# A decode block on one Trainium2 core: part of the scores and wider value products on VectorE, a maximum of its own for each key group, heads normalised together

## The chip, the core and the metric

The kernel runs on one core of a Trainium2 chip. Its engines are TensorE (PE; its weight loads are PEld), VectorE (DVE), ScalarE (ACT), GpSimd (POOL) and SyncE (SP), which issues nearly all transfers here; 16 DMA engines move the data from HBM. The metric is the device time of one execution in microseconds. Where a time is given for the kernel before, it is the median of three runs; the profile is of one execution.

## The reference

One decoding step of a transformer block for a batch of B = 2, with one token each, all in fp32:

```python
x = A_x                                          # (2, 1, 448)
q = (layernorm(x) @ wq) -> 16 heads of 256
scores = einsum("bhqd,bhkd->bhqk", q, k_cache) * 256 ** -0.5     # 8192 keys
p = softmax(scores)
h = x + einsum("bhqk,bhkd->bhqd", p, v_cache) @ wo
n = layernorm(h)
out = h + ((n @ w_gate) * (n @ w_up)) @ w_down   # 448 -> 1792 -> 448
```

The caches are what is large: 2 x 16 x 8192 x 256 numbers each for K and V, 537 MB together. Every one of these numbers is used once.

## The kernel before, in words

The work is cut into 32 items, one per head and batch row, in the order item i = 2 h + b. For each, one 8 MB tile of K (`kt`, 64 KB per partition) and one of V (`vt`, the same) come in. K lies with the 256 feature dimensions as two chunks of 128 partitions and the 8192 keys as G = 4 groups of GK = 2048. V lies with partition = key group and value row r (R = 32), and NO = 8 columns of 2048 keys each.

There is one K buffer (pool `kbuf`), and there are two V buffers (pool `vbuf`). All loads are issued by SyncE in program order: wq, K0, V0, K1, V1, and so on (L84, L91). SyncE waits at each until its buffer is free, and everything behind stands behind it: K of item i + 1 waits until every reader of K of item i is done, V of item i + 1 until the products of item i - 1 are done. The order on every engine is the program's own; there is no scheduler.

For an item:

- `scores` (L201 to L209): 32 matmuls, 4 key tiles of 512 x 2 chunks x 4 groups. The four groups write to four blocks of 32 partitions of `s`, which holds the scores of all 8192 keys as 128 x 2048 in four PSUM banks. The 32 rows of a group are equal, as the query is repeated.
- VectorE takes the maximum along the keys (L242), PE transposes the 128 maxima (L244), VectorE takes their maximum (L246), PE spreads it to all partitions (L248), ScalarE copies it (L250).
- ScalarE computes p = exp(s - maximum), with the sum along the way (L252).
- VectorE multiplies each of the 8 columns of V by p and sums, in one instruction each with an accumulator (L259). These go back into the V buffer and are not read again; the sums are in `oacc`.

After both batch rows of a head `head_out` (L211 to L223) sums over partitions, divides by the sum of the exponentials and places the head in `oT`. It is issued after the scores of the next item.

After the last item, the K buffer takes wo in five loads, one V buffer the gate and up weights (`gu_t`, two and three loads), the other w_down (`wd_t`, five loads) (L265 to L278). Then: the output projection with wo (L292), the residual and the layer norm (L303 to L335), gate (L347), its scaling on ScalarE by the inverse variance (L348), up (L349), the product (L353), four transposes (L357), the product with w_down (L364), two copies and the output. g_ps and u_ps are two banks of one tile, `ff`.

Of the kernel before, what the change touches and what calls it, by code (L numbers as in the profile page):

```python
# [8 lines left out]
F32 = mybir.dt.float32  # L9
# [39 lines left out]
def tile_decode_block(  # L49
# [122 lines left out]

    qT = const.tile([P, 2, G, 2, 2, B], F32, name="qT")
    q_ps = ps_s.tile([P, 4, MM], F32, tag="s", name="q_ps")
    q_sb = one.tile([P, 2, MM], F32, tag="p", name="q_sb")
    for k in range(2):
        project(
            q_ps[:, k], wq_t, HD, (MM,) * 4, [k * BATCH + g * MM for g in range(4)],
# [9 lines left out]
            q_ps[:, 2 + k].rearrange("p (n g b r) -> p n g b r", n=4, g=G, b=B)[..., 0],  # L188
        )

    def queries(h):
        q = one.tile([P, 2, B, R], F32, tag="q", name=f"q_{h}")
        nc.scalar.activation(
            q.rearrange("p c b r -> p (c b) r"),
            qT.rearrange("p k g j c b -> p (k g j) (c b)")[:, h, :, None]
            .to_broadcast([P, 2 * B, R]),
            AF.Copy,
        )
        return q

    def scores(s, q, b, kt):  # L201
        for j in range(GK // MM):
            at = slice(j * MM, (j + 1) * MM)
            for c in range(2):
                for g in range(G):
                    nc.tensor.matmul(  # L206
                        s[g * R : (g + 1) * R, at], q[:, c, b, :], kt[:, c, g, at],
                        start=(c == 0), stop=(c == 1),
                    )  # L209

    def head_out(h, oacc, lsum):  # L211
        l_ps = ps_m.tile([P, B], F32, tag="sm", name=f"l_ps_{h}")
        nc.tensor.matmul(l_ps, ones, lsum, start=True, stop=True)  # L213
        rl = work.tile([P, B], F32, tag="rl", name=f"rl_{h}")
        nc.vector.reciprocal(rl, l_ps)  # L215
        oT_ps = ps_m.tile([P, B, 2], F32, tag="sm", name=f"oT_ps_{h}")
        for r in range(G):
            nc.tensor.matmul(
                oT_ps[r * R : (r + 1) * R], gsum, oacc[:, :, r::G], start=True, stop=True
            )  # L220
        nc.vector.tensor_mul(
            oT[:, h].rearrange("p c b -> p b c"), oT_ps, rl[:, :, None].to_broadcast([P, B, 2])
        )  # L223

    q_now = queries(0)
    last = None

    for i in range(NQ):
        h, b = divmod(i, B)
        kt = load_k(b, h)  # L230
        vt = load_v(b, h, 2 if i == NQ - 1 else 1)
        if b == 0:
            oacc = work.tile([P, B, NO], F32, tag="oacc", name=f"oacc_{h}")
            lsum = work.tile([P, B], F32, tag="lsum", name=f"lsum_{h}")

        s = ps_s.tile([P, GK], F32, tag="s", name=f"s_{i}")
        scores(s, q_now, b, kt)
        if last is not None:
            head_out(*last)
            last = None  # L240
        m = work.tile([P, 1], F32, tag="m", name=f"m_{i}")
        nc.vector.tensor_reduce(m, s, axis=AX.X, op=ALU.max)  # L242
        mT = ps_m.tile([1, P], F32, tag="sm", name=f"mT_{i}")
        nc.tensor.transpose(mT, m, ident)  # L244
        nm = work.tile([1, 1], F32, tag="nm", name=f"nm_{i}")
        nc.vector.tensor_reduce(nm, mT, axis=AX.X, op=ALU.max, negate=True)  # L246
        nb_ps = ps_m.tile([P, 1], F32, tag="sm", name=f"nb_ps_{i}")
        nc.tensor.matmul(nb_ps, ones[0:1, :], nm, start=True, stop=True)  # L248
        nb = work.tile([P, 1], F32, tag="nb", name=f"nb_{i}")
        nc.scalar.activation(nb, nb_ps, AF.Copy, scale=float(R))  # L250
        p = one.tile([P, GK], F32, tag="p", name=f"p_{i}")
        nc.scalar.activation(p, s, AF.Exp, bias=nb, scale=1.0, accum_out=lsum[:, b : b + 1])  # L252

        if b == B - 1 and h + 1 < H:
            q_now = queries(h + 1)

        for o in range(NO):
            v = vt[:, o, :]
            nc.vector.scalar_tensor_tensor(  # L259
                v, v, 1.0, p, op0=ALU.mult, op1=ALU.mult, accum_out=oacc[:, b, o : o + 1]  # L260
            )
        if b == B - 1:
            last = (h, oacc, lsum)
# [8 lines left out]
    def load_ff(t, w, cuts):  # L272
        for a, z in zip((0,) + cuts, cuts + (NF * D,)):
            nc.sync.dma_start(t[:, a:z], w[:, a:z])
# [7 lines left out]
    hm_ps = [ff[:, at, : 2 * P].rearrange("p (n k) -> p n k", k=P) for at in (2, 0)]  # L282
    ya_ps, yb_ps = ff[:B, 3, :YC], acc_ps[32 : 32 + B, :YC]
    for t in (g_ps, u_ps):
        nc.vector.memset(t[2 * 32 :, FG[2] :], 0.0)
# [9 lines left out]
                )  # L295

    project_out(range(WO_CUTS[1]))
    head_out(*last)
# [14 lines left out]
    hT = const.tile([P, DC, B], F32, name="hT")  # L313
    nc.vector.tensor_add(hT, xT, hT_ps)
    xc = center(hT, "h")
    for rows, c, to in LAYOUT:
        k = rows.stop - rows.start
        nc.vector.tensor_copy(  # L318
            xr[rows, to],
            xc[rows, c][:, :, :, None].to_broadcast([k, c.stop - c.start, B, 16]),  # L320
        )
# [14 lines left out]
    for ps, a, z in ((ya_ps, 0, YC), (yb_ps, YC, D)):  # L336
        at = a
        while at < z:
            c, k = divmod(at, P)
            n = min(P - k, z - at)  # L340
            nc.tensor.matmul(  # L341
                ps[:, at - a : at - a + n], hT[:, c, :], ident[:, k : k + n],
                start=(at == a), stop=False, skip_group_check=True,
            )
            at += n

    project_ff(g_ps, wg_t)  # L347
    nc.scalar.activation(g_sb, g_ps, AF.Copy, scale=rv)  # L348
    project_ff(u_ps, wu_t)  # L349
    hmT = const.tile([P, 4, 4, B], F32, name="hmT")  # L350
# [25 lines left out]
def pack(np, inputs):  # L376


    x = np.asarray(inputs["A_x"]).reshape(B, D).T
    last = x[3 * P :]  # L380
    got = {
        "x": np.concatenate(
            [x[: 3 * P].reshape(3, P, B).transpose(1, 0, 2).reshape(P, 3 * B),
             np.concatenate([last, last], axis=0)], axis=1
        )
    }
    k = np.asarray(inputs["A_k_cache"]).reshape(B, H, SK, 2, P)
    got["kc"] = np.ascontiguousarray(k.transpose(0, 1, 4, 3, 2)).reshape(B, H, P, 2 * SK)
# [45 lines left out]
```

## Time and profile before

| | us |
|---|---|
| median of three runs (1306.52 to 1307.53) | 1307.19 |
| the profiled execution's own time | 1306.09 |
| its span, first to last instruction | 1304.3 |
| VectorE busy | 663.4 |
| TensorE matmuls busy | 365.3 |
| ScalarE busy | 79.6 |
| mean granted TensorE clock, as a share | 0.631 |
| bytes moved by DMA (MB) | 561.59 |

The page is read with the program's names: `k<-in_kc_dram` is a K load, `s<-k,q` a score matmul, `v<-v,p` a value product. In a row of a group stand line, engine, operation, output and inputs, shapes and the count; then busy time and mean ns of one; then the engine's idle time just before these instructions and what ended it. In a row of a timeline stand start, duration, engine, line and operation, and in brackets the idle time before and its releaser. One matmul of fp32 shows as two records. In a row of a table of windows stand the window, its length, the busy time of PE, PEld, VectorE, ScalarE and GpSimd, then the granted TensorE clock, the share of the DMA engines and GB/s.

### The profile page before, as it was taken

The numbers are of one execution on the slowest core, as the hardware profiler recorded it, in microseconds if no ns is written. First come the engines' busy times: TensorE is split into PE (matmuls) and PEld (weight loads), VectorE is DVE, ScalarE is ACT, GpSimd is POOL, SyncE is SP. The second block draws the span as 40 slices with busy tenths as digits, with TensorE's granted clock in tenths as the row PEclk, the third lists the DMA queues.
The fourth block names the chain that finished last, engine by engine and source line by source line (L and its number), as shares of the span: only waits on it lengthen the run. The fifth ranks groups of instructions, "written<-read, shape, count | busy, mean of one in ns | idle before, by whom it ended". The sixth has DMA issues, their size and how long they took to land.

```text
span 1304.3 us, 6274 instructions
## 1 busy us (share of the span) xinstructions
PE 365.3 (28%) x2592; PEld 116.9 (9%) x2592; DVE 663.4 (51%) x648; ACT 79.6 (6%) x119; POOL 0.8 (0%) x7
## 2 busy tenths in 40 slices
PE   3333212332212233211232211323321233321247
PEld 1000000010000001000010000101000010100012
DVE  0246564445565445655444656444556544556552
ACT  0100000000000000000000000000000000000000
POOL 0000000000000000000000000000000000000000
PEclk9666566666556666656666655666655666655669
DMA  9999999999999999999999999999999999999998
GB/s 418 421 446 421 446 423 444 425 442 427 440 428 437 433 434 435 432 435 434 432 437 430 439 428 441 426 443 424 445 422 446 423 445 422 445 424 444 424 425 340
DMA packets 11841, 561.59 MB, mean 431 GB/s; under 512 B 1443, under 2 KB 1573, under 8 KB 2597
## 3 DMA queue, kind: packets, MB, share of 16 engines
q1 hardware_dynamic: 11668, 561.19, 99.5%
q8 instruction: 20, 0.33, 0.1%
q14 instruction: 9, 0.07, 0.0%
q10 hardware_dynamic: 144, 0.00, 0.0%
HBM read 561.19 MB, written 0.00 MB: 430 GB/s over the span
## 4 chain that ended last, share of the span: by engine, by line
DMA 75%; PE 24%; issue 0%; DVE 0%; SPq 0%; ACT 0%; ACTq 0%; DVEq 0%
DMA k<-in_kc_dram 73%; PE s L206 23%; DMA wo_t<-in_wo_dram 2%; PE ff_ps L167 1%; PE ff_ps L364 0%; SPq L267 0%; PE hT_ps L309 0%; PE acc_ps L292 0%; PE ff_ps L357 0%; PE l_ps L213 0%; DVE tail L353 0%; ACT tail L348 0%; DVE tail L303 0%; DVE xr L318 0%; PE acc_ps L341 0%
## 5 line engine op out<-in xcount | busy, mean ns | idle before, releaser
L259 DVE SCALAR_TENSOR_TENSOR v<-v,p 128x2048 f32<-128x2048 f32 x256 | 569.0, 2288 | 215.6 <-DMA v<-in_vc_dram 212.6
L206 PE MATMUL s<-k,q 128*32 128x512 f32 x2048 | 294.4, 739 | 804.2 <-DMA k<-in_kc_dram 804.2
L242 DVE TENSOR_REDUCE m<-s 128x1 f32<-128x2048 f32 x32 | 73.2, 2287 | 190.2 <-PE s L206 190.2
L206 PEld LDWEIGHTS s<-k,q 128*32 128x32 f32 x2048 | 80.9, 133 | 991.5 <-issue 991.5
L215 DVE RECIPROCAL rl<-l_ps 128x2 f32<-128x2 f32 x16 | 2.7, 171 | 166.7 <-PE l_ps L213 166.7
L250 ACT ACTIVATE nb<-nb_ps 128x1 f32<-128x1 f32 x32 | 5.5, 172 | 1148.3 <-PE nb_ps L248 1148.3
L252 ACT ACTIVATE p<-s,nb 128x2048 f32<-128x2048 f32 x32 | 63.0, 1968 | 1.0
L244 PE MATMUL mT<-ident,m 128*1 128x128 f32 x32 | 9.8, 306 | 79.4 <-DVE m L242 79.4
L259 DVE DVE_READ_ACCUMULATOR v<-v,p 128x1 f32 x256 | 21.3, 83 | 0.0
L248 PE MATMUL nb_ps<-nm,ones 1*128 1x1 f32 x64 | 15.2, 303 | 11.8 <-DVE nm L246 11.8
L246 DVE TENSOR_REDUCE nm<-mT 1x1 f32<-1x128 f32 x32 | 8.9, 278 | 12.7 <-PE mT L244 12.7
L248 PEld LDWEIGHTS nb_ps<-nm,ones 1*128 1x128 f32 x64 | 12.4, 241 | 19.1 <-DVE nm L246 19.1
L292 PE MATMUL acc_ps<-wo_t,oT 128*2 128x448 f32 x64 | 9.2, 632 | 14.6 <-DMA wo_t<-in_wo_dram 14.6
L244 PEld LDWEIGHTS mT<-ident,m 128*1 128x1 f32 x32 | 2.5, 79 | 96.1 <-DVE m L242 96.1
L167 PE MATMUL q_ps<-wq_t,xr 128*32 128x512 f32 x64 | 9.2, 727 | 2.3 <-DMA wq_t<-in_wq_dram 1.9
L167 PE MATMUL ff_ps<-gu_t,xr 128*32 128x384 f32 (+1 forms) x64 | 8.7, 633 | 0.9 <-ACT tail L348 0.9
L118 DVE TENSOR_REDUCE sum_h_x<-xT 128x2 f32<-128x6 f32 x1 | 0.2, 159 | 14.4 <-DMA xT<-in_x_dram 14.4
L186 DVE COPY qT<-q_ps 128x32 f32<-128x32 f32 x2 | 0.4, 191 | 12.0 <-PE q_ps L183 12.0
L252 ACT ACTIVATION_READ_ACCUMULATOR p<-s,nb 128x1 f32 x32 | 6.2, 193 | 0.0
L213 PE MATMUL l_ps<-lsum,ones 128*128 128x2 f32 x32 | 6.1, 262 | 0.0
L213 PEld LDWEIGHTS l_ps<-lsum,ones 128*128 128x128 f32 x32 | 4.8, 188 | 13.3 <-issue 13.3
L353 DVE TENSOR_TENSOR tail<-ff_ps,tail 128x256 f32<-128x256 f32 x2 | 0.8, 420 | 9.8 <-PE ff_ps L167 9.8
(69 smaller groups left out, 60.8 us busy)
## 6 DMA issues: line engine op xcount, KB each, us to landing
v<-in_vc_dram SPq DMA_DIRECT2D x2, 4096.0 KB, 37.8
wq_t<-in_wq_dram SPq DMA_DIRECT2D x1, 7168.0 KB, 19.4
wo_t<-in_wo_dram SPq DMA_DIRECT2D x1, 2688.0 KB, 16.2
wo_t<-in_wo_dram SPq DMA_DIRECT2D x1, 2240.0 KB, 21.2
gu_t<-in_B_w_gate_dram SPq DMA_DIRECT2D x1, 1792.0 KB, 28.9
gu_t<-in_B_w_up_dram SPq DMA_DIRECT2D x1, 1792.0 KB
wd_t<-in_wd_dram SPq DMA_DIRECT2D x2, 896.0 KB, 19.8
wo_t<-in_wo_dram SPq DMA_DIRECT2D x1, 1344.0 KB, 23.9
```

Of the source, the lines that this page charges most:

```text
L167: nc.tensor.matmul(ps[32 * g : 32 * g + 32, : wide[g]], xs.rearrange("p b r -> p (b r)"), w[:, at : at + wide[g]], start=(c == 0), stop=(c ...
L206: nc.tensor.matmul(s[g * R : (g + 1) * R, at], q[:, c, b, :], kt[:, c, g, at], start=(c == 0), stop=(c == 1),)
L213: nc.tensor.matmul(l_ps, ones, lsum, start=True, stop=True)
L215: nc.vector.reciprocal(rl, l_ps)
L242: nc.vector.tensor_reduce(m, s, axis=AX.X, op=ALU.max)
L244: nc.tensor.transpose(mT, m, ident)
L246: nc.vector.tensor_reduce(nm, mT, axis=AX.X, op=ALU.max, negate=True)
L248: nc.tensor.matmul(nb_ps, ones[0:1, :], nm, start=True, stop=True)
L250: nc.scalar.activation(nb, nb_ps, AF.Copy, scale=float(R))
L252: nc.scalar.activation(p, s, AF.Exp, bias=nb, scale=1.0, accum_out=lsum[:, b : b + 1])
L259: nc.vector.scalar_tensor_tensor(v, v, 1.0, p, op0=ALU.mult, op1=ALU.mult, accum_out=oacc[:, b, o : o + 1])
L292: nc.tensor.matmul(acc_ps[32 * j : 32 * j + B, :], oT[:, h, c, :], wo_t[:, k * D : (k + 1) * D], start=(h < 2), stop=(h >= H - 2),)
```

## The change

1. **Own maximum by key group.** The maximum (now negated, `nm`) of each partition is used for that partition's exponential as it is. The transpose, the second maximum, the spreading matmul and ScalarE's copy are gone from every item. Since each of the four groups now has its own reference point, `weights` makes factors exp(overall minimum of `nm` taken against the own) over the sum, and `weigh` multiplies `oacc` by them.
2. **Fifteen heads normalised at once.** `weights` and `weigh` run once for the first 30 items (EARLY), ahead of and behind the value products of item 29, and once for the last two. `turn` and `heads_out` place 15 heads in `oT` together. `head_out` is gone.
3. **VectorE part of the scores.** For items i < 30 with i % 3 == 1 (ten items), the upper 128 feature dimensions are laid out by the host with partition = (key group, r) and four strips of 2048 keys. VectorE multiplies the first strip by its query column and adds the other three (one TENSOR_SCALAR, three SCALAR_TENSOR_TENSOR, in place in the K buffer). PE does the lower chunk (16 matmuls) and then adds the strip's sum over r with four matmuls against a block matrix of ones. `qd` holds these query columns, made once at the start with four matmuls.
4. **Wide V products.** For items i < 30, n = 4, 4 or 8 columns (i % 3 = 0, 1, 2) are multiplied by p in one TENSOR_TENSOR and summed in one TENSOR_REDUCE; the other 8 - n stay as before.
5. **The end.** u_ps has a PSUM bank of its own. The last piece of up's weights is cut in two (four loads). The gate's matmuls stand ahead of the variance's, and the matmuls that bring h into the output's accumulators ahead of the copies to `xr`.

```diff
+EARLY = NQ - B
+WIDE = (4, 4, 8)
+def by_vector(i):
+    return i < EARLY and i % 3 == 1
...
+    qd = const.tile([P, G, NQ], F32, name="qd")
+    for o in range(G):
+        nc.tensor.matmul(qd_ps[:, o, :]..., spread[:, o]..., qT...[:, :, 1, :], start=True, stop=True)
+    nc.vector.tensor_copy(qd, qd_ps)
...
-    def scores(s, q, b, kt):
+    def scores(s, q, i, kt):
+        upper = kt[:, 1]
+        if by_vector(i):
+            nc.vector.tensor_scalar(
+                upper[:, 0], upper[:, 0], qd[:, 0, i : i + 1], None, op0=ALU.mult
+            )
+            for o in range(1, G):
+                nc.vector.scalar_tensor_tensor(
+                    upper[:, 0], upper[:, o], qd[:, o, i : i + 1], upper[:, 0],
+                    op0=ALU.mult, op1=ALU.add,
+                )
+        for at in tiles:
+            for c in range(1 if by_vector(i) else 2):
                 for g in range(G):
                     nc.tensor.matmul(s[g * R : (g + 1) * R, at], q[:, c, i % B, :], kt[:, c, g, at], ...)
+        if by_vector(i):
+            for at in tiles:
+                nc.tensor.matmul(s[:, at], block, upper[:, 0, at], start=False, stop=True, ...)
...
+    def weights(a, z):
+        nc.tensor.transpose(nmT, nm[:, a:z], ident)
+        nc.vector.tensor_reduce(low, nmT, axis=AX.X, op=ALU.min)
+        nc.vector.tensor_scalar(diag, ident[:n, :n], low, None, op0=ALU.mult)
+        nc.tensor.matmul(all_ps, ones[:n, :], diag, start=True, stop=True)
+        nc.vector.scalar_tensor_tensor(w, all_ps, float(R), nm[:, a:z], op0=ALU.mult, op1=ALU.subtract)
+        nc.scalar.activation(w, w, AF.Exp)
+        nc.vector.tensor_mul(lw, ls[:, a:z], w)
+        nc.tensor.matmul(l_ps, ones, lw, start=True, stop=True)
+        nc.vector.reciprocal(rl, l_ps)
+        nc.vector.tensor_mul(w, w, rl)
+    def weigh(a, z, w):
+        nc.vector.tensor_mul(oacc[:, a:z], oacc[:, a:z], w[:, :, None].to_broadcast([P, z - a, NO]))
...
-        nc.vector.tensor_reduce(m, s, axis=AX.X, op=ALU.max)
-        nc.tensor.transpose(mT, m, ident)
-        nc.vector.tensor_reduce(nm, mT, axis=AX.X, op=ALU.max, negate=True)
-        nc.tensor.matmul(nb_ps, ones[0:1, :], nm, start=True, stop=True)
-        nc.scalar.activation(nb, nb_ps, AF.Copy, scale=float(R))
-        nc.scalar.activation(p, s, AF.Exp, bias=nb, scale=1.0, accum_out=lsum[:, b : b + 1])
+        nc.vector.tensor_reduce(nm[:, i : i + 1], s, axis=AX.X, op=ALU.max, negate=True)
+        nc.scalar.activation(p, s, AF.Exp, bias=nm[:, i : i + 1], scale=1.0, accum_out=ls[:, i : i + 1])
...
+        n = WIDE[i % 3] if i < EARLY else 0
+        if n:
+            v = vt[:, :n, :]
+            nc.vector.tensor_mul(v, v, p[:, None, :].to_broadcast([P, n, GK]))
+            nc.vector.tensor_reduce(oacc[:, i, :n], v, axis=AX.X, op=ALU.add)
+        for o in range(n, NO):
             nc.vector.scalar_tensor_tensor(v, v, 1.0, p, ..., accum_out=oacc[:, i, o : o + 1])
...
-    load_ff(wu_t, wu, (2 * F, 3 * F))
+    load_ff(wu_t, wu, (2 * F, 3 * F, 3 * F + FG[0]))
-    g_ps, u_ps = ff[:, 0], ff[:, 1]
+    g_ps = ff[:, 0]
+    u_ps = ps_1.tile([P, MM], F32, name="u_ps")
...
+    project_ff(g_ps, wg_t)
     nc.tensor.matmul(var, sr..., ones[:, 0:1], start=True, stop=True)
     nc.vector.tensor_scalar(ve, var, R / D, EPS, op0=ALU.mult, op1=ALU.add)
     nc.vector.reciprocal(rv, ve)
-    project_ff(g_ps, wg_t)
     nc.scalar.activation(g_sb, g_ps, AF.Copy, scale=rv)
     project_ff(u_ps, wu_t)
```

How VectorE's order moves, around items 2, 3 and 4 (v_0_297, v_1_366 and v_0_425 before). Before:

```order
L242 TENSOR_REDUCE m_344<-s_301 128x1
L246 TENSOR_REDUCE nm_348<-mT_346 1x1
L259 SCALAR_TENSOR_TENSOR v_0_297,oacc_299<-v_0_297,p_354 128x2048 x8
L242 TENSOR_REDUCE m_401<-s_368 128x1
L246 TENSOR_REDUCE nm_405<-mT_403 1x1
L259 SCALAR_TENSOR_TENSOR v_1_366,oacc_299<-v_1_366,p_411 128x2048 x8
L215 RECIPROCAL rl_464<-l_ps_462 128x2
L221 TENSOR_TENSOR oT<-oT_ps_466,rl_464 128x2x2
L242 TENSOR_REDUCE m_472<-s_429 128x1
```

and now, with the same items as v_0_282, v_1_324 and the K of item 4, k_0_370:

```order
L321 TENSOR_REDUCE nm<-s_284 128x1 [waits PE_49]
L340 TENSOR_TENSOR v_0_282<-v_0_282,p_318 128x16384 [waits DMAHW7_49,Activation_49]
L341 TENSOR_REDUCE oacc<-v_0_282 128x8 [waits DVE_49]
L321 TENSOR_REDUCE nm<-s_326 128x1 [waits PE_49]
L340 TENSOR_TENSOR v_1_324<-v_1_324,p_360 128x8192 [waits DMAHW1_49,Activation_49]
L341 TENSOR_REDUCE oacc<-v_1_324 128x4 [waits DVE_49]
L344 SCALAR_TENSOR_TENSOR v_1_324,oacc<-v_1_324,p_360 128x2048 x4
L243 TENSOR_SCALAR k_0_370<-k_0_370,qd 128x2048 [waits DMAHW6_49,DMAHW2_49,DMAHW0_49]
L247 SCALAR_TENSOR_TENSOR k_0_370<-k_0_370,qd 128x2048 [waits DVE_49] x3
L321 TENSOR_REDUCE nm<-s_374 128x1 [waits PE_49]
```

The four vector instructions on K of item 4 stand behind all value products of item 3 and ahead of item 4's own maximum.

PE's order at item 4, before (s_429) and now (s_374). Before:

```order
L206 MATMUL s_429<-k_0_423,q_413 32x512 [waits DMAHW2_49,PE_49,Activation_49]
L206 MATMUL s_429<-k_0_423,q_413 32x512 x31
L213 MATMUL l_ps_462<-lsum_300,ones 128x2
L218 MATMUL oT_ps_466<-oacc_299,gsum 32x4 [waits DVE_49] x4
L244 MATMUL mT_474<-ident,m_472 1x128 [waits DVE_49]
L248 MATMUL nb_ps_478<-nm_476,ones 128x1 [waits DVE_49]
```

and now:

```order
L255 MATMUL s_374<-k_0_370,q_362 32x512 [waits DMAHW2_49,PE_49,Activation_49]
L255 MATMUL s_374<-k_0_370,q_362 32x512 x15
L261 MATMUL s_374<-k_0_370,block 128x512 [waits DVE_49]
L261 MATMUL s_374<-k_0_370,block 128x512 x3
L255 MATMUL s_412<-k_1_408,q_362 32x512 [waits DMAHW4_49,Activation_49]
```

The last readers of K of item 4 are now matmuls that wait for VectorE.

More of the change, by code (lines that the diff above doesn't have):

```diff
@@ L111, in tile_decode_block @@
     oT = const.tile([P, H, 2, B], F32, name="oT")
+    block = const.tile([P, P], F32, name="block")
+    nc.gpsimd.memset(block, 0.0)
+    for g in range(G):
+        nc.gpsimd.memset(block[g * R : (g + 1) * R, g * R : (g + 1) * R], 1.0)
+    nm = const.tile([P, NQ], F32, name="nm")
+    ls = const.tile([P, NQ], F32, name="ls")
+    oacc = const.tile([P, NQ, NO], F32, name="oacc")
     acc_ps = ps_1.tile([P, D], F32, name="acc_ps")
@@ L189, in tile_decode_block @@
         )
+    qd = const.tile([P, G, NQ], F32, name="qd")
+    qd_ps = ps_m.tile([P, G, NQ], F32, tag="sm", name="qd_ps")
+    for o in range(G):
+        nc.tensor.matmul(
+            qd_ps[:, o, :].rearrange("p (n b) -> p n b", b=B),
+            spread[:, o].rearrange("p g r -> p (g r)"),
+            qT.rearrange("p k g j c b -> p (k g j) c b")[:, :, 1, :],
+            start=True, stop=True,
+        )
+    nc.vector.tensor_copy(qd, qd_ps)
     def queries(h):
@@ L205, in scores @@
                 for g in range(G):
                     nc.tensor.matmul(
-                        s[g * R : (g + 1) * R, at], q[:, c, b, :], kt[:, c, g, at],
-                        start=(c == 0), stop=(c == 1),
-                    )
[L211 to L214, printed above, removed]
-        nc.vector.reciprocal(rl, l_ps)
-        oT_ps = ps_m.tile([P, B, 2], F32, tag="sm", name=f"oT_ps_{h}")
+                        s[g * R : (g + 1) * R, at], q[:, c, i % B, :], kt[:, c, g, at],
@@ L223, in head_out, with heads_out @@
+    def heads_out(a, z, oT_ps):
+        nc.vector.tensor_copy(
+            oT[:, a // B : z // B].rearrange("p h c b -> p h b c"),
+            oT_ps.rearrange("p (h b) c -> p h b c", b=B),
         )
     q_now = queries(0)
-    last = None
     for i in range(NQ):
@@ L315, in tile_decode_block @@
     xc = center(hT, "h")
+    for ps, a, z in ((ya_ps, 0, YC), (yb_ps, YC, D)):
+        at = a
+        while at < z:
+            c, k = divmod(at, P)
+            n = min(P - k, z - at)
+            nc.tensor.matmul(
+                ps[:, at - a : at - a + n], hT[:, c, :], ident[:, k : k + n],
+                start=(at == a), stop=False, skip_group_check=True,
+            )
+            at += n
     for rows, c, to in LAYOUT:
@@ L387, in pack @@
     k = np.asarray(inputs["A_k_cache"]).reshape(B, H, SK, 2, P)
-    got["kc"] = np.ascontiguousarray(k.transpose(0, 1, 4, 3, 2)).reshape(B, H, P, 2 * SK)
+    kc = np.ascontiguousarray(k.transpose(0, 1, 4, 3, 2)).reshape(B, H, P, 2 * SK)
+    for h, b in (divmod(i, B) for i in range(NQ) if by_vector(i)):
+        upper = k[b, h, :, 1].reshape(G, GK, G, R).transpose(0, 3, 2, 1)
+        kc[b, h, :, SK:] = upper.reshape(P, SK)
+    got["kc"] = kc
     v = np.asarray(inputs["A_v_cache"]).reshape(B, H, G, GK, NO, R)
```

86 lines of the change are left out of this document (51 added, 35 removed).

## The prediction

> **What bounds the kernel now.** I read the page first: engine shares, the row of DMA shares, the queues and the chain that ended last.
>
> ```profile
> PE 365.3 (28%) x2592; PEld 116.9 (9%) x2592; DVE 663.4 (51%) x648; ACT 79.6 (6%) x119; POOL 0.8 (0%) x7
> DMA  9999999999999999999999999999999999999998
> q1 hardware_dynamic: 11668, 561.19, 99.5%
> q8 instruction: 20, 0.33, 0.1%
> DMA 75%; PE 24%; issue 0%; DVE 0%; SPq 0%; ACT 0%; ACTq 0%; DVEq 0%
> ```
>
> No compute engine is near full, and the DMA engines are busy from the first slice to the last. The chain calls 24% of the span PE, though; the SyncE waits and one period of the loop show how this goes together.
>
> ```profile
> SPq L84 <- PE s L206: 149.4, 16, 10.1
> ...
> 79.81 9.96 PE L206 MATMUL s<-k,q 128*32 128x512 f32 x64 [26.88 <-DMA k<-in_kc_dram]
> ...
> 89.83 0.33 SPq L84 DMA_DIRECT2D k<-in_kc_dram  x1
> ...
> 99.10 2.29 DVE L259 SCALAR_TENSOR_TENSOR v<-v,p 128x2048 f32<-128x2048 f32 x1 [6.34 <-DMA v<-in_vc_dram]
> 101.32 0.08 DVE L259 DVE_READ_ACCUMULATOR v<-v,p 128x1 f32 x1
> ...
> 118.42 9.43 PE L206 MATMUL s<-k,q 128*32 128x512 f32 x64 [25.02 <-DMA k<-in_kc_dram]
> ```
>
> K lands and its scores start at 79.81, V lands by 99.10, the next K by 118.42: 19.3 us each, 38.6 us per item, without a pause. There is one K buffer, so the next K load is issued when the scores end, at 89.83, 10.0 us after K landed. It costs nothing only because V is still on its way for another 9.3 us. **That lead of 9.3 us is the one slack on the path.** What the change does to it decides; the V buffer comes free 8 steps of 2.21 after 99.10, long before it is wanted.
>
> **The change, part by part.** Call the time of a vector-scored item's scores starting T (items 1, 4, ... 28, ten of them), the item before it (wide 4) A, the one before that (wide 8) C. In an unbroken stream V of A is there at T - 19.3 and V of C at T - 57.9.
>
> Prices come from these groups of instructions:
>
> ```profile
> L259 DVE SCALAR_TENSOR_TENSOR v<-v,p 128x2048 f32<-128x2048 f32 x256 | 569.0, 2288 | 215.6 <-DMA v<-in_vc_dram 212.6 <-ACT p L252 3.0
> L242 DVE TENSOR_REDUCE m<-s 128x1 f32<-128x2048 f32 x32 | 73.2, 2287 | 190.2 <-PE s L206 190.2
> L353 DVE TENSOR_TENSOR tail<-ff_ps,tail 128x256 f32<-128x256 f32 x2 | 0.8, 420 | 9.8 <-PE ff_ps L167 9.8
> L121 DVE SCALAR_TENSOR_TENSOR sum_h_h<-hT,sum_h_h 128x2 f32<-128x2 f32 x1 | 0.2, 162 | 0.0
> L118 DVE TENSOR_REDUCE sum_h_h<-hT 128x2 f32<-128x6 f32 x1 | 0.2, 159 | 0.0
> L318 DVE COPY xr<-xc_h 64x32 f32<-64x32 f32 x2 | 0.3, 172 | 0.0
> L323 DVE COPY tail<-sum_sq_h 128x128 f32<-128x128 f32 x1 | 0.2, 227 | 0.0
> ```
>
> *Wide V products.* From 2 to 2048 elements a two-input instruction grows from 162 to 2288 ns, 1.04 ns per element; a reduction from 159 (6 elements) to 2287, the same. So 8192 elements cost 0.16 + 8.51 = 8.67 us and 16384 cost 17.2. Four columns now need a product pass and a reduction, 17.3 us, where four fused instructions at a step of 2.21 (99.10 to 101.32) needed 8.85. A then has 17.3 + 8.9 = 26.2 us of products, C 34.4, before 17.7. The other end, as four instructions of 2.29 per 8192, is 9.15. I take 8.67: the rows' growth is per element, and a wide pass has no starts in between.
>
> *Vector scores.* One TENSOR_SCALAR and three dependent SCALAR_TENSOR_TENSORs of 2048. The three are 3 x 2.29 = 6.9. The first has one tensor input, as the COPY rows have: 55 ns for 96 elements more, 0.57 ns each, so 0.17 + 1.16 = 1.3 us; at worst 2.29. Together 8.2.
>
> *Block matmuls.* Four of 512 columns, two passes each as in the 64 records for 32 score matmuls. What a pass costs depends on the clock:
>
> ```profile
> 52.00:54.00 2.00, 0.58 (x2) 0.50 (x2) 0.28 (x1) 1.01 (x2) 0.00 (x0) 0.50 1.21 524
> ...
> 79.80:85.50 5.70, 5.69 (x28) 1.55 (x32) 0.00 (x0) 0.00 (x0) 0.00 (x0) 0.50 1.19 517
> 85.50:89.83 4.33, 4.27 (x40) 1.07 (x32) 0.00 (x0) 0.00 (x0) 0.00 (x0) 0.98 1.12 484
> ...
> 84.05 0.22 PEld L206 LDWEIGHTS s<-k,q 128*32 128x32 f32 x4 [0.63 <-issue]
> 84.91 0.22 PEld L206 LDWEIGHTS s<-k,q 128*32 128x32 f32 x4 [0.63 <-issue]
> 85.72 0.13 PEld L206 LDWEIGHTS s<-k,q 128*32 128x32 f32 x4 [0.59 <-issue]
> 86.15 0.13 PEld L206 LDWEIGHTS s<-k,q 128*32 128x32 f32 x4 [0.30 <-issue]
> ...
> 195.61 8.39 PE s L206 x64
> ```
>
> In these windows (the third number from the right is the granted clock) the clock is back at 0.50 within 3 us of the scores' end and stays so for the first 5.7 us of the next burst. A pass of 512 columns is 0.86 us cold (84.05 to 84.91) and 0.43 warm (85.72 to 86.15). Sixteen warm passes would be 6.9; the bursts take 8.39 to 10.0, so cold starts cost 1.5 to 3.1, in the middle 2.3. PE does the lower half's 8 passes by T + 6.8, then idles about 9 us for VectorE and is cold again: block = 8 x 0.43 + 2.3 = 5.8 us, bounds 4.95 and 6.55. The weight loads of 128 x 128 (188 ns at L213) I take as hidden, as the scores' are; if not, 8 x 0.19 = 1.5 more.
>
> The Trainium skill ("TensorE: Matmul & The Clock Gate", Part 1) has a cold array warm up after about 3.4 us of sustained work; by that the block would be 3.4 + 4 x 0.43 = 5.1 us and the whole estimate some 7 us lower. The rows above disagree with it here: 5.7 us at half clock.
>
> *Exponential.* The own maximum per key group takes the transpose, the second reduction, a small matmul and a copy out of the chain. What stays is read from the last item:
>
> ```profile
> 1254.95 1.97 ACT L252 ACTIVATE p<-s,nb 128x2048 f32<-128x2048 f32 x1
> ...
> 1257.04 2.29 DVE L259 SCALAR_TENSOR_TENSOR v<-v,p 128x2048 f32<-128x2048 f32 x1 [2.97 <-ACT p L252]
> ```
>
> that is 2.09 us from its start to the products. VectorE's wait before the products was ended by V's DMA, not by p (the 99.10 row, 6.34 us), so the shortened chain gains nothing by itself.
>
> *The lead of an empty queue.*
>
> ```profile
> 0.74 0.40 SPq L100 DMA_DIRECT2D wq_t<-in_wq_dram  x1
> ...
> 1.20 38.30 DMA k<-in_kc_dram
> ...
> 1302.01 0.33 SPq L370 DMA_DIRECT2D out_dram<-tail  x1
> ```
>
> The wq load (7168 KB) and the first K (8192 KB) go into an empty queue at 0.74 and are there at 39.5: 38.8 us for bytes worth 15360/8192 x 19.3 = 36.2, so 2.6 us of lead. The output, 2.3 us from issue to the span's end, gives the lower bound, 2.0 with the issue taken off. The Trainium skill ("DMA: Bandwidth & Descriptors", on fixed and variable cost) gives about 2.0 us fixed per DMA; with it the sum below would be 6 us smaller. The traced load decides.
>
> *The sum for one round of three items.* C's products run T - 57.9 + 34.4 = T - 23.5. A's maximum, whose scores had ended at about T - 29.4, waits for them: T - 21.2; p at T - 19.1, V of A at T - 19.3, so A's products start at T - 19.1 and end at T + 7.1. VectorE stands in program order, so the vector scores wait behind them: T + 7.1 to T + 15.3. Block until T + 21.1. Only then is the K buffer free. The next K lands 2.6 + 19.3 us later, with 0.1 to the matmul, at T + 43.1; in the unbroken stream it was T + 38.6. **A hole of 4.5 us in the load stream per vector-scored item.** Its V, queued behind that K on SyncE, is late by as much. Round item 1 no C goes before: 4.3. Nothing gives it back: the stream has no other slack, and the other items' VectorE work fits (2.3 + 34.4 and 2.3 + 26.2 in periods of 38.6; the vector item's V products end at T + 21.1 + 2.3 + 2.1 + 26.2 = T + 51.7, before C's scores end). Ten holes: 45 us.
>
> *Normalising.* The 30-column chain of small instructions falls between the maximum of item 29 and its V, where VectorE waits 6 us (the 99.10 row); the one for the last two items takes the place of the old maximum chain. Nothing on the path: without that cover a dozen instructions of 0.16 us and three trips to PE, some 3 us once.
>
> *The end.*
>
> ```profile
> L274 SPq DMA_DIRECT2D wd_t<-in_wd_dram x5: 327/328/328, 1275.8 to 1285.4; - x5
> ...
> DMA to landing us min/median/max: 15.1/19.3/20.9
> ...
> 1284.42 5.07 PE L167 MATMUL ff_ps<-gu_t,xr 128*32 128x384 f32 x32
> 1290.36 3.67 PE L167 MATMUL ff_ps<-gu_t,xr 128*32 128x512 f32 x32 [0.87 <-ACT tail L348]
> ...
> 1301.57 0.38 DVE L368 COPY tail<-ff_ps 2x224 f32<-2x224 f32 x1 [5.21 <-PE acc_ps L364]
> ```
>
> The gate could start 2 us earlier and up need not wait 0.87 us for ScalarE. But the last piece of w_down lands at 1285.4 + 15.1 = 1300.5, and the copy-out starts at 1301.57; between them the last chunk's matmuls need about 0.5. So the new head start is worth 0.5 us, bounds 0 and 0.7. One more load of up does not stretch the queue: the pieces are issued 10 us and more ahead.
>
> *Total.* The profiled execution took 1306.1 (span 1304.3, so 1.8 around it), 1.1 under the median of the runs. 1306.1 + 45 - 0.5 = 1351. Low end of the bounds: block -0.85, lead -0.6, TENSOR_SCALAR -0.25: a hole of 2.8, 1334. High end: wide passes at 9.15 (+0.5 for each of the six of A and C), TENSOR_SCALAR at 2.29 (+1.0), block +0.75, loads of weights +1.5: a hole of 10.7, 1413.
>
> **The rivals.**
> *No hole, no change: about 1305.6.* The K buffer would have to be free by T + 16.6, 4.5 us earlier. That happens if the wide passes run at two elements per cycle: A's products would end near T - 1, the vector scores at T + 8.3, the block at T + 14. For it: the COPY rows do run at that rate. Against: the only product of two tensors with many elements, L353, takes 420 ns for 256, and both reduction and fused rows stand at 1.04 ns.
> *Faster: 1300.* Some K intervals are longer than 38.6 without any wait showing:
>
> ```profile
> 581.98 9.76 PE s L206 x64
> 591.79 30.20 DMA k<-in_kc_dram
> 622.13 8.50 PE s L206 x64
> ```
>
> 40.15 here. From 39.63 to 1241.68 the 31 intervals sum to 1202, 5.3 over 31 x 38.6. If fetching instructions (the q8 row) disturbs the stream, a program with some 460 matmul records fewer gives part of it back: at most 5.3 + 0.5, 1300.3. It decides only if no hole opens and over half of the 5.3 comes back. Against: they are merely 18% of 2592.
> *Twice the hole: 1390.* If weight loads are exposed, the TENSOR_SCALAR runs at 2.29 and wide passes cost as short ones do, holes of 8 us and more open.
>
> **How the numbers follow.** A hole of 2.5 to 7 us per vector item (1331 to 1376): 0.70, and 1351 is its middle. A small hole, 1309 to 1331: 0.08. Larger: 0.08. No hole: 0.09. Faster: 0.05. A measurement of this kernel tells about 0.2%, 2.6 us, from no change. So slower 0.86, same 0.09, faster 0.05. The range 1311 to 1390 leaves out the last two, and the ends of the small and the large hole, 0.18 in all; the likeliest case's own is 1331 to 1376.
>
> **What would show it.** In the new profile: ten K landings some 43 us after the one before, all behind items 1, 4, ... 28, the others 38.6; SyncE's K issue there waiting for the block matmuls until about 21 us after K landed (10 now), and DMA slices falling below 9. VectorE busy near 1065 us. TENSOR_TENSOR 8192 at 8.7, TENSOR_SCALAR 1.3, three further ones 2.29, block 5 to 6.5 at clock 0.5 first. Wrong would be a block that ends by T + 17, a lead far from 2.6, or VectorE done with A's products before T.

## The result and the profile after

The changed kernel takes 1367.82 us (median, 1364.16 to 1368.72) beside 1307.15 us of the kernel before on the same chip (1306.34 to 1307.53): a ratio of 1.0458, 95% interval 1.0442 to 1.0474. It is 60.7 us slower. The prediction was 1351 with a range of 1311 to 1390. The profiled execution took 1368.11 us with a span of 1366.3, that is 62.0 more span than before.

The page of the changed kernel, engine shares, DMA slices, the queue of the loads, and the chain that ended last:

```profile
PE 363.4 (27%) x2130; PEld 111.0 (8%) x2130; DVE 1071.3 (78%) x382; ACT 74.3 (5%) x89; POOL 1.4 (0%) x12
DMA  9989998999899899989989998999999899989998
q1 hardware_dynamic: 11812, 561.19, 95.6%
DMA 56%; DVE 28%; PE 13%; issue 2%; another core or an unknown queue 1%; ACT 0%; SPq 0%; DVEq 0%; ACTq 0%
```

The bytes are the same, the row of DMA slices now has eights spread evenly along it, and VectorE, which had no share in the chain before, holds 28% of it. At 78% of the span it is still not busy throughout; it is on the path in certain places only. SyncE's waits say which:

```profile
SPq L99 <- DVE k L247: 399.9, 10, 45.8
SPq L99 <- PE s L255: 192.6, 21, 10.0
SPq L99 <- PE s L261: 62.8, 10, 6.7
```

The columns are the time in us in total, the number of waits and the longest. For 21 K loads the wait ends with the score matmuls (L255), as before. For ten it ends with VectorE's strips (L247) and then with the block matmuls (L261), these 6.3 us on average. One round from the timeline, items 6 to 10 (rows of other operations are left out at the dots):

```profile
303.84 8.69 DVE L340 TENSOR_TENSOR v<-v,p 128x8192 f32<-128x8192 f32 x1 [3.31 <-DMA v<-in_vc_dram]
...
323.18 5.63 PE L255 MATMUL s<-k,q 128*32 128x512 f32 x32 [31.39 <-DMA k<-in_kc_dram]
...
327.80 2.29 DVE L344 SCALAR_TENSOR_TENSOR v<-v,p 128x2048 f32<-128x2048 f32 x1
...
330.02 1.28 DVE L243 TENSOR_SCALAR k<-k,qd 128x2048 f32<-128x2048 f32 x1
...
338.52 6.56 PE L261 MATMUL s<-k,block 128*128 128x512 f32 x8 [9.71 <-DVE k L247]
...
345.11 0.33 SPq L99 DMA_DIRECT2D k<-in_kc_dram  x1
...
367.24 9.22 PE L255 MATMUL s<-k,q 128*32 128x512 f32 x64 [22.17 <-DMA k<-in_kc_dram]
...
386.56 17.23 DVE L340 TENSOR_TENSOR v<-v,p 128x16384 f32<-128x16384 f32 x1 [7.75 <-DMA v<-in_vc_dram]
...
405.93 8.65 PE L255 MATMUL s<-k,q 128*32 128x512 f32 x64 [29.48 <-DMA k<-in_kc_dram]
...
426.44 8.69 DVE L340 TENSOR_TENSOR v<-v,p 128x8192 f32<-128x8192 f32 x1 [3.20 <-DMA v<-in_vc_dram]
...
445.79 5.76 PE L255 MATMUL s<-k,q 128*32 128x512 f32 x32 [31.21 <-DMA k<-in_kc_dram]
```

This is the round of the prediction with T = 323.18. VectorE is free of item 6's products at 330.02 (T + 6.8), the strips end at 338.5 (T + 15.3), the block at 345.1 (T + 21.9), and SyncE issues the next K in that instant. K is there 22.1 us later. So 44.1 us lie between the scores of items 7 and 8 where 38.6 are a full stream. The rows after it show a second, smaller loss: V of item 8 and K of item 9 come after 19.3 and 19.4 us, but V of item 9 after 20.5 (405.93 to 426.44).

All 31 intervals between one item's scores and the next, sorted in this way, make the table by which the experiments are read. *Holes* is what the ten intervals behind items 1, 4, ... 28 have over 38.6 us each; *others* is the same for the other 21; *end* runs from the last item's scores to the end of the span.

| span and its parts, us | first scores | holes | others | end | span |
|---|---|---|---|---|---|
| before | 39.6 | 0.6 | 4.8 | 62.6 | 1304.3 |
| after | 40.0 | 50.9 | 14.7 | 64.1 | 1366.3 |
| difference | 0.4 | 50.3 | 9.9 | 1.4 | 62.0 |

### The profile page after: what moved, and what is told of

It is laid out like the page before. It is cut to its first block, busy times and chain, and to the rows that moved or that the text cites. A ratio compares the mean times of both kernels' runs of the same rounds, so it can differ in the third digit from the quotient of the medians.

```text
span 1366.3 us, 5044 instructions
## 1 busy us (share of the span) xinstructions
PE 363.4 (27%) x2130; PEld 111.0 (8%) x2130; DVE 1071.3 (78%) x382; ACT 74.3 (5%) x89; POOL 1.4 (0%) x12
## 4 chain that ended last, share of the span: by engine, by line
DMA 56%; DVE 28%; PE 13%; issue 2%; another core or an unknown queue 1%; ACT 0%; SPq 0%; DVEq 0%; ACTq 0%
DMA k<-in_kc_dram 27%; DMA v<-in_vc_dram 27%; DVE v L340 8%; PE s L255 7%; DVE oacc L341 7%; DVE v L344 6%; DVE k L247 5%; PE s L261 5%; DMA gu_t<-in_B_w_up_dram 2%; DVE k L243 1%; DVE nm L321 0%; PE u_ps L189 0%; PE ff_ps L450 0%; ACT p L325 0%
## 5 line engine op out<-in xcount | busy, mean ns | idle before, releaser
L255 PE MATMUL s<-k,q 128*32 128x512 f32 x1728 | 255.7, 755 | 845.4 <-DMA k<-in_kc_dram 845.4
L340 DVE TENSOR_TENSOR v<-v,p 128x8192 f32<-128x8192 f32 (+1 forms) x30 | 346.1, 11537 | 136.3 <-DMA v<-in_vc_dram 107.9
L341 DVE TENSOR_REDUCE oacc<-v 128x4 f32<-128x8192 f32 (+1 forms) x30 | 345.9, 11531 | 1.0
L344 DVE SCALAR_TENSOR_TENSOR v<-v,p 128x2048 f32<-128x2048 f32 x96 | 214.0, 2287 | 2.1 <-ACT p L325 2.1
L255 PEld LDWEIGHTS s<-k,q 128*32 128x32 f32 x1728 | 69.8, 135 | 1029.4 <-issue 1029.4
L321 DVE TENSOR_REDUCE nm<-s 128x1 f32<-128x2048 f32 x32 | 73.2, 2289 | 88.1 <-PE s L261 63.3
L325 ACT ACTIVATE p<-s,nm 128x2048 f32<-128x2048 f32 x32 | 63.0, 1968 | 1194.6 <-DVE nm L321 1194.6
L261 PE MATMUL s<-k,block 128*128 128x512 f32 x80 | 62.3, 950 | 97.3 <-DVE k L247 97.3
L247 DVE SCALAR_TENSOR_TENSOR k<-k,qd 128x2048 f32<-128x2048 f32 x30 | 70.6, 2352 | 1.1
L261 PEld LDWEIGHTS s<-k,block 128*128 128x128 f32 x80 | 23.9, 315 | 135.4 <-DVE k L247 96.0
L379 PE MATMUL acc_ps<-wo_t,oT 128*2 128x448 f32 x64 | 10.3, 708 | 12.6 <-DMA wo_t<-in_wo_dram 12.6
L243 DVE TENSOR_SCALAR k<-k,qd 128x2048 f32<-128x2048 f32 x10 | 12.8, 1284 | 0.0
L189 PE MATMUL q_ps<-wq_t,xr 128*32 128x512 f32 x64 | 10.3, 799 | 1.3 <-DVE xn L173 1.0
L344 DVE DVE_READ_ACCUMULATOR v<-v,p 128x1 f32 x96 | 8.1, 84 | 0.0
```

What stands on the lines that cost most here:

```text
L189: nc.tensor.matmul(ps[32 * g : 32 * g + 32, : wide[g]], xs.rearrange("p b r -> p (b r)"), w[:, at : at + wide[g]], start=(c == 0), stop=(c ...
L243: nc.vector.tensor_scalar(upper[:, 0], upper[:, 0], qd[:, 0, i : i + 1], None, op0=ALU.mult)
L247: nc.vector.scalar_tensor_tensor(upper[:, 0], upper[:, o], qd[:, o, i : i + 1], upper[:, 0], op0=ALU.mult, op1=ALU.add,)
L255: nc.tensor.matmul(s[g * R : (g + 1) * R, at], q[:, c, i % B, :], kt[:, c, g, at], start=(c == 0), stop=(c == 1), skip_group_check=True,)
L261: nc.tensor.matmul(s[:, at], block, upper[:, 0, at], start=False, stop=True, skip_group_check=True,)
L321: nc.vector.tensor_reduce(nm[:, i : i + 1], s, axis=AX.X, op=ALU.max, negate=True)
```

## The experiments

The theory of the prediction, called the hole theory: only the late release of the K buffer behind vector-scored items costs time, some 5 us each. Its rivals are that the added VectorE load costs by itself (load theory), and that the way of scoring on VectorE and the block of ones costs by itself (detour theory).

**Vector scores off.** Everything else of the change stays.

```diff
 def by_vector(i):
-    return i < EARLY and i % 3 == 1
+    return False
```

> The changed kernel, with all scores on TensorE again and K in its old layout; the wide products, the own maxima and the new end stay. VectorE loses some 85 of its 1071 us. Hole theory (the K buffer comes free too late because the vector scores wait behind the wide products of the item before): no holes, K landings 38.6 us apart, 1306 to 1310 us. Load theory (wide passes or VectorE's higher load slow the stream of loads themselves): wide passes are some 335 of the 410 us added, so about four fifths of the loss stays, near 1355. Besides, each round of the changed kernel lost a further 1.2 us at one V landing: if that follows a queue that ran empty it is gone here; if it comes from the wide passes it stays and the time is near 1318.

1306.5 us, ratio 0.9998 (0.9989 to 1.0008).

```profile
PE 339.8 (26%) x2370; PEld 98.1 (8%) x2370; DVE 988.9 (76%) x342; ACT 74.3 (6%) x89; POOL 1.4 (0%) x12
DMA  9999999999999999999999999999999999999997
```

VectorE is busy 326 us longer than before, and nothing happens: all slices are full again, holes 1.5, others 2.5. The load theory falls.

**Wide products off.** The vector scores stay; VectorE does A's products in eight fused steps as before.

```diff
-WIDE = (4, 4, 8)
+WIDE = (0, 0, 0)
```

> The changed kernel without wide products (all eight columns fused as before); the vector scores stay. Hole theory: the item before ends its products 17.8 us after its V, 1.5 us ahead of K, the vector scores take 8.4 and the block 6.6, so the K buffer is free 15 us after K's scores start; with 22.1 us to the next scores that is 37.2, inside 38.6: no hole, 1306 to 1310 us. Detour theory (vector scores and block alone are too long for one K buffer): 1360 and more. Load theory: about a fifth of the loss, near 1319.

1306.14 us, ratio 0.9996 (0.9986 to 1.0005). The timeline at item 4 shows why:

```profile
195.42 1.29 DVE L243 TENSOR_SCALAR k<-k,qd 128x2048 f32<-128x2048 f32 x1 [1.50 <-issue]
195.47 5.50 PE L255 MATMUL s<-k,q 128*32 128x512 f32 x32 [29.14 <-DMA k<-in_kc_dram]
...
203.92 3.70 PE L261 MATMUL s<-k,block 128*128 128x512 f32 x8 [2.95 <-DVE k L247]
...
207.65 0.33 SPq L99 DMA_DIRECT2D k<-in_kc_dram  x1
...
234.13 8.38 PE L255 MATMUL s<-k,q 128*32 128x512 f32 x64 [26.51 <-DMA k<-in_kc_dram]
```

VectorE stands ready when K lands, the strips run beside the matmuls, and K is issued 12.2 us after the scores' start, while V is still under way. The detour theory falls: scoring on VectorE costs nothing here when VectorE is free. Here PE had idled only 2.95 us before the block, and the block took 3.70 us, not 5.8; so did seven of the ten, and the other three took 5.40. In all ten K was issued earlier than the 15 us expected.

Neither half of the change costs anything alone that these runs can tell: both intervals hold 1. What costs is that one stands ahead of the other in VectorE's order. Two kernels keep both halves and all of VectorE's work, and change only what stands there.

**Wide products moved to other items.** The item ahead of a vector-scored one (remainder 0) gets none, the vector-scored one itself eight.

```diff
-WIDE = (4, 4, 8)
+WIDE = (0, 8, 8)
```

> The changed kernel with 0, 8, 8 wide columns in place of 4, 4, 8: the same number of wide columns in a round of three items, the same VectorE time, but none in the item ahead of a vector-scored one. Hole theory: that item's products end 17.8 us after its V; the item behind starts on time; no hole, 1306 to 1310 us. Load theory and detour theory: 1368 as before, since work and detour are unchanged.

**Strips between the products.** The load of the vector-scored item's K keeps its place in SyncE's order, but its strips are issued in the item ahead, between that item's wide passes and its four fused products.

```diff
             nc.vector.tensor_reduce(oacc[:, i, :n], v, axis=AX.X, op=ALU.add)
+        if by_vector(i + 1):
+            kt_next = load_k((i + 1) % B, (i + 1) // B)
+            strips(i + 1, kt_next)
         for o in range(n, NO):
```

> The changed kernel with the four vector instructions on K placed between the wide passes and the four fused products of the item before, in place of behind them; all work is the same. Hole theory: wide passes end 1.9 us ahead of K, the vector scores run at once, block free at 15 us: no hole, 1306 to 1310 us. Load theory and detour theory: 1368.

1305.65 us, ratio 0.9992 (0.9982 to 1.0001), with VectorE busy for 1069.1 us, and 1305.24 us, ratio 0.9992 (0.9982 to 1.0001), with 1070.7. The second at item 4:

```profile
195.72 1.29 DVE L243 TENSOR_SCALAR k<-k,qd 128x2048 f32<-128x2048 f32 x1 [1.61 <-DMA k<-in_kc_dram]
...
204.23 5.40 PE L264 MATMUL s<-k,block 128*128 128x512 f32 x8 [2.27 <-DVE k L247]
...
209.66 0.33 SPq L99 DMA_DIRECT2D k<-in_kc_dram  x1
```

K is issued 13.9 us after it landed, within the T + 16.6 of the prediction. With the same instructions as in the slow kernel and VectorE as busy, 62 us are gone by the order of a few of them. That settles that the hole is one of order. Neither is clear of the kernel before: the loads still set the time.

**PE kept warm.** Ten matmuls into an unused bank stand ahead of the block's; their results are thrown away.

```diff
+            for _ in range(FILL):              # 10
+                nc.tensor.matmul(u_ps, block, kt[:, 0, 0, :MM], start=True, stop=True, ...)
             for at in tiles:
                 nc.tensor.matmul(s[:, at], block, upper[:, 0, at], start=False, stop=True, ...)
```

> The changed kernel with ten matmuls of 512 columns in front of the block matmuls of a vector-scored item; their results are thrown away, they only keep TensorE working while VectorE does the strips. Hole theory with the block's cold clock as a term: the block falls from 6.2 to about 3.6 us, each of the ten holes by some 2.6, 1368 to about 1342 us. If the clock did not matter (the block bound by its weight loads): 1368. If the added matmuls end behind the strips: above 1368.

1342.48 us, ratio 1.0269 (1.0253 to 1.0285).

```profile
319.69 5.24 PE L257 MATMUL s<-k,q 128*32 128x512 f32 x32 [29.94 <-DMA k<-in_kc_dram]
...
324.86 8.85 PE L263 MATMUL u_ps<-k,block 128*128 128x512 f32 x20
...
335.02 3.70 PE L265 MATMUL s<-k,block 128*128 128x512 f32 x8 [1.31 <-DVE k L249]
...
360.77 8.61 PE L257 MATMUL s<-k,q 128*32 128x512 f32 x64 [22.05 <-DMA k<-in_kc_dram]
```

The block takes 3.70 us instead of 6.56 and the interval is 41.1 instead of 44.1. Holes fall from 50.9 to 26.3: the cold restart of PE was 2.5 us of each hole. Others stay at 15.6, though the holes are half as long.

**The kernel before with long scores.** No part of the change: items 1, 4, ... 28 do their score matmuls three times over (the repeats give the same scores), so the K buffer is held for 22.7 us with no VectorE work added. This tells whether the loss in the other intervals belongs to VectorE's work or to the emptied queue.

```diff
-        for j in range(GK // MM):
+        for j in [j for _ in range(3 if i < NQ - B and i % 3 == 1 else 1) for j in range(GK // MM)]:
```

> The kernel before with nothing of the change, but items 1, 4, ... 28 do their score matmuls three times over (same result), so that the K buffer comes free some 9.3 + 2 x 6.9 = 23 us after the scores start. No VectorE work is added. Hole theory: 23 + 22.1 - 38.6 = 6.5 us per hole, ten of them, 1372 us. If each emptied queue costs a further 1.2 us at a later landing: 1380 to 1384. If only VectorE's load slowed the changed kernel: 1307.

1374.94 us, ratio 1.0517 (1.0503 to 1.0531), between the two expectations.

```profile
202.97 22.73 PE L206 MATMUL s<-k,q 128*32 128x512 f32 x192 [25.46 <-DMA k<-in_kc_dram]
...
247.71 8.82 PE L206 MATMUL s<-k,q 128*32 128x512 f32 x64 [17.94 <-DMA k<-in_kc_dram]
...
287.65 9.32 PE L206 MATMUL s<-k,q 128*32 128x512 f32 x64 [27.69 <-DMA k<-in_kc_dram]
...
326.26 9.22 PE L206 MATMUL s<-k,q 128*32 128x512 f32 x68 [24.91 <-DMA k<-in_kc_dram]
```

The hole (44.74 us), then an interval of 39.94, then 38.61. Holes 59.0, others 13.9. The further loss comes with the emptied queue, and needs none of the change's VectorE work.

**Two and six wide columns ahead of the vector scores.** One number sets the length of the hole. A wide pass takes 4.43, 8.69 and 12.96 us for 2, 4 and 6 columns, so two columns more lengthen the two passes by 8.5 us and save two fused steps of 2.21: 4.1 us. This tells a loss per emptied queue from one that grows with the hole.

```diff
-WIDE = (4, 4, 8)
+WIDE = (2, 4, 8)        # and (6, 4, 8)
```

> The changed kernel with 2 wide columns in place of 4 in the items 0, 3, 6, ..., those ahead of a vector-scored one; items behind them as they are. Their products then take 2 x 4.4 + 6 x 2.21 = 22.2 us in place of 26.3. Hole theory: each of the ten holes shrinks from 5.2 to 1.1 us: 11 us in all. If each emptied queue costs a fixed 0.8 to 1.2 us besides, whatever its length: 1325 to 1329 us. If that further loss is a share of the hole: 1318 to 1320.

> The same with 6 wide columns there: 2 x 13.0 + 2 x 2.21 = 30.4 us of products, holes of 9.3 us, 93 in all. With a fixed further loss per emptied queue: 1407 to 1412 us; if it grows with the hole: 1414 and more. If the stream had further slack behind the hole: below 1400.

1324.14 us, ratio 1.0131 (1.0116 to 1.0146), and 1408.03 us, ratio 1.0777 (1.0759 to 1.0795). The kernel with two, from item 4 on:

```profile
208.88 6.58 PE L261 MATMUL s<-k,block 128*128 128x512 f32 x8 [6.03 <-DVE k L247]
...
237.67 9.20 PE L255 MATMUL s<-k,q 128*32 128x512 f32 x64 [22.22 <-DMA k<-in_kc_dram]
...
276.30 8.66 PE L255 MATMUL s<-k,q 128*32 128x512 f32 x64 [29.43 <-DMA k<-in_kc_dram]
...
316.06 5.82 PE L255 MATMUL s<-k,q 128*32 128x512 f32 x32 [31.10 <-DMA k<-in_kc_dram]
```

One of its ten K loads behind vector-scored items that took longer than the others, behind item 19:

```profile
804.07 0.33 SPq L99 DMA_DIRECT2D k<-in_kc_dram  x1
...
829.11 8.74 PE L255 MATMUL s<-k,q 128*32 128x512 f32 x64 [25.07 <-DMA k<-in_kc_dram]
```

The kernel with six:

```profile
225.35 6.09 PE L261 MATMUL s<-k,block 128*128 128x512 f32 x8 [14.04 <-DVE k L247]
...
253.68 8.95 PE L255 MATMUL s<-k,q 128*32 128x512 f32 x64 [22.23 <-DMA k<-in_kc_dram]
```

| | holes, ten | others | end |
|---|---|---|---|
| two wide columns | 10.1 | 13.1 | 62.8 |
| PE kept warm | 26.3 | 15.6 | 62.7 |
| four (the change) | 50.9 | 14.7 | 64.1 |
| long scores | 59.0 | 13.9 | 64.0 |
| six wide columns | 93.6 | 12.4 | 63.0 |

From four to six columns the holes grow by 42.7, that is 4.3 us for each, where VectorE's instructions make 4.1: there the hole is a plain sum. From two to four they grow by 40.8, and that this is 4.1 each as well is in part luck. With two columns K is issued 4.6 us earlier on average (17.1 us after the scores' start instead of 21.7), as the block is shorter too (5.75 us instead of 6.23). But two of the ten K loads took 23.5 and 25.0 us from their issue to the next scores instead of some 22.1, and these 4.3 us take most of that away again.

Others stay between 12.4 and 15.6 while the holes go from 1.0 to 9.4 us each. So the further loss does not grow with the hole: it is 0.8 to 1.1 us for each of ten over the 4.8 us that the kernel before has without any, and 1.3 in the kernel with two columns when the 4.3 us are counted to it. "Emptied queue" is to be taken loosely: with two columns K is issued 16.4 to 18.0 us after the scores' start, and with PE kept warm after 18.9 to 19.6, when V, which needs 19.3, is mostly still on its way. What these kernels share is a load that is issued by less than its lead ahead.

**The new end alone,** on the kernel before: u's own bank, four loads of up, the gate and the matmuls on h moved forward.

```diff
-    load_ff(wu_t, wu, (2 * F, 3 * F))
+    load_ff(wu_t, wu, (2 * F, 3 * F, 3 * F + FG[0]))
...
+    u_ps = ps_1.tile([P, MM], F32, name="u_ps")
...
+    project_ff(g_ps, wg_t)
     var = ps_m.tile([P, 1], F32, tag="sm", name="var_h")
...
-    project_ff(g_ps, wg_t)
```

> The kernel before with only the new end (own bank for up, gate ahead of the variance, four loads of up). In the changed kernel's profile the gate was done early, TensorE idled 2.4 us for up's weights, and up then ran at half clock, 5.3 us in place of 3.7. Clock theory: up ends 0.5 to 1.5 us later than before, 1307.5 to 1308.5 us. As predicted: 1306.6, half a microsecond less. No difference that can be told: between the two.

1306.4 us, ratio 0.9995 (0.9986 to 1.0004): no difference that can be told. From the timeline and the chain that ended last:

```profile
1289.72 1.91 PE L167 MATMUL u_ps<-gu_t,xr 128*32 128x512 f32 x16 [2.02 <-DMA gu_t<-in_B_w_up_dram]
...
1302.04 0.33 SPq L370 DMA_DIRECT2D out_dram<-tail  x1
```

```profile
1278.00 19.38 DMA wd_t<-in_wd_dram
...
1297.42 0.35 PE ff_ps L364
```

PE begins up early and waits for its weights, later for w_down's; the output is issued at 1302.04, before at 1302.01. The head start is taken whole by the loads.

## Why the prediction was right, and where it was mis-sized

**The mechanism** was right: the K buffer held too long behind VectorE's order, ten holes, SyncE's issue at about T + 21 and V late by as much. Vector scores off, wide products off, and the two kernels that only move work all take the holes away; long scores bring them back without VectorE.

**The terms of the hole** against the trace:

```profile
L340 DVE TENSOR_TENSOR v<-v,p 128x8192 f32<-128x8192 f32 x20 | 173.9, 8693 | 57.3 <-DMA v<-in_vc_dram 28.9 <-ACT p L325 28.4
L341 DVE TENSOR_REDUCE oacc<-v 128x8 f32<-128x16384 f32 x10 | 172.2, 17220 | 0.3
L247 DVE SCALAR_TENSOR_TENSOR k<-k,qd 128x2048 f32<-128x2048 f32 x30 | 70.6, 2352 | 1.1
L243 DVE TENSOR_SCALAR k<-k,qd 128x2048 f32<-128x2048 f32 x10 | 12.8, 1284 | 0.0
L261 PE MATMUL s<-k,block 128*128 128x512 f32 x80 | 62.3, 950 | 97.3 <-DVE k L247 97.3
```

| term of one round | predicted | measured |
|---|---|---|
| end of A's products after T | 7.1 | 6.8 |
| wide pass of 8192 / 16384 | 8.67 / 17.2 | 8.69 / 17.22 |
| TENSOR_SCALAR and three fused strips | 8.2 | 8.5 |
| block | 5.8 | 6.23 (mean; 5.1 to 6.7) |
| K issued to scores | 22.0 | 22.0 (mean; 21.8 to 22.4) |
| hole | 4.5 | 5.1 (mean) |

Most of the miss within the hole is the block, which was put in the middle of its bounds of 4.95 and 6.55; the 0.3 us by which A's products ended earlier and the 0.3 us by which the strips were longer cancel. After some 10 us of idling PE starts cold. In windows of 0.1 us the granted clock stays at 0.5 for 2.9 to 6.1 us from the block's start, 5.2 on average over the ten; eight of the ten blocks took 6.1 to 6.7 us, the other two 5.1 and 5.2.

The Trainium skill's 3.4 us of warm-up ("TensorE: Matmul & The Clock Gate", Part 1), weighed in the prediction, would have made the block 5.1 by the estimate there. That is what these two took, and the trace's row of 5.7 us at half clock was nearer to the rest. The prediction did not carry that row to its end: 5.7 us are 6.6 of the eight passes at 0.86, the other 1.4 at 0.43 make 0.6, together 6.3, where it took 5.8 from what whole bursts lose.

From K's issue to the next scores the ten K loads behind vector-scored items took 21.8 to 22.4 us, 22.0 on average, so the lead of 2.6, read off the first loads, holds there. The 2.0 of "DMA: Bandwidth & Descriptors" in the Trainium skill, which the page gives for DMAs on the GpSimd path, is short for these loads of SyncE.

**The step that failed** is the silent other half of the sentence "Nothing gives it back: the stream has no other slack", namely that nothing further is lost either. The sum took the 21 other intervals as they were. They have 9.9 us more, and this is the largest part of what was missed: of 17.5 us in the span (62.0 measured against 44.5), the holes are 5.3 (50.3 against 45), the others 9.9, the end 1.9, the start 0.4. That the time still lies inside the range, and even inside the likeliest case's own, is luck in this respect: the width was made of the hole's terms and held nothing for such a loss.

**The end** was put at -0.5 (0 to -0.7) and is +1.4. The timeline and the windows of the changed kernel:

```profile
1346.40 1.91 PE L189 MATMUL ff_ps<-gu_t,xr 128*32 128x512 f32 x16 [1.17 <-DMA gu_t<-in_B_w_gate_dram]
...
1351.04 5.32 PE L189 MATMUL u_ps<-gu_t,xr 128*32 128x512 f32 x32 [2.42 <-DMA gu_t<-in_B_w_up_dram]
```

```profile
1348.00:1351.00 3.00, 0.62 (x4) 0.30 (x2) 0.32 (x2) 0.69 (x1) 0.00 (x0) 1.00 0.94 398
1351.00:1354.00 3.00, 2.96 (x18) 1.25 (x22) 0.00 (x0) 0.00 (x0) 0.00 (x0) 0.54 1.05 424
```

With the gate done earlier PE waits 2.4 us for up's weights; the clock falls from 1.00 to 0.54 and up takes 5.3 us instead of the 3.7 of the kernel before. But this is not the edit's fixed price. Among the kernels with the new end, up took 5.32 in this one, with vector scores off and with the strips between the products (ends 64.1, 64.3 and 63.3). It took about 3.9 with wide products off or moved, with PE kept warm, with two and six wide columns and with the new end alone (ends 62.6 to 63.0). In the first three the gate ran in two pieces of 1.91 us, 1.2 us apart as it waited for its own weights; in the others it ran in one burst of 4.6 to 6.0 us, partly at half clock. Whether that decides it was not tested. Long scores, with the old end, ends at 64.0 although its up took 3.63, its gate being at half clock for longer; so the end is not settled by up alone.

**The rivals.** *No hole* rested on wide passes at two elements per cycle: 8.69 us for 8192 is 1.06 ns per element. Only TENSOR_SCALAR is faster, 1284 ns for 2048, 0.63 each. *Faster by fewer instructions*: what all 31 intervals have over 38.6 is 5.4 before (the prediction's 5.3), 4.0 with vector scores off, 5.3 with wide products off, 3.7 with wide products moved and 4.8 with the strips between. If something comes back, it is under 2 us, and no time differs from before by more than the noise. *Twice the hole* did not come; its upper end for the block was met by some of the ten, but by the clock and not by weight loads: with PE kept warm, the same weights loaded, the block took 3.70.

## What to carry to other kernels

Where a buffer has a single copy, write down when its last reader must be done for the next load to be issued in time (here 16.6 us after its own landing, the lead subtracted), and check for each engine that reads it what stands ahead in its program order at that moment; an engine's busy share says nothing about it (1070 us of VectorE's work cost 62 us in one order and nothing in another). Work that holds back a load belongs ahead of work that has slack, and a load queue that runs dry cost its hole here and some 1 us more behind it.

## What the runs showed of the hardware

- After a load queue ran dry and was restarted, one of the next landings, at times two, came late: by 0.8 to 1.9 us in all behind each of the ten restarts of the changed kernel (20.5 us instead of 19.3 in the round shown). With ten restarts the other intervals lose 12.4 to 15.6 us in all, without any 2.5 to 5.1, for holes from 1.0 to 9.4 us and with or without VectorE's work. The kernel before has it at its own start too (first K's scores at 39.63, first V at 60.47: 20.8 us). What in the DMA makes it was not found.
- PE's clock can fall after the pause that it follows, when PE is at work again. One block of the kernel with wide products off, behind 3.50 us of idling:

```profile
901.30:902.40 1.10, 1.09 (x3) 0.62 (x4) 0.00 (x0) 0.00 (x0) 0.00 (x0) 1.00 0.96 417
902.40:905.80 3.40, 3.40 (x6) 1.35 (x5) 0.00 (x0) 0.00 (x0) 0.00 (x0) 0.50 0.93 405
```

  In 15 blocks of the kernels with wide products off, with wide products moved and with the strips between, behind pauses of 2.0 to 3.5 us, the clock was 1.0 at the block's start, fell to 0.5 between 0.1 and 1.4 us later and stayed there for some 3.4 us; each block took 5.4 us instead of 3.70. In the other seven with wide products off, behind 2.8 to 3.2 us, it stayed at 1.0. So the length of the pause alone does not decide it, and what does was not tested. With four and with two wide columns, behind pauses of 4.5 to 10.3 us, the block began at 0.5 and took 5.1 to 6.7 us.
- A fused instruction with its multiplier from a tensor and no accumulator took 2352 ns, one with a constant and an accumulator 2288; which of the two makes the difference was not tested.
